# Attention on one core: K and V of a pair of heads loaded in 2 KB rows in one row order, one transfer each

## Chip, cores and metric

The kernel runs on one core of one Trainium2 chip. The metric is device time in microseconds (us) of one launch; the span in the profile is the time from the first to the last instruction of one profiled execution. "PE" is TensorE, "ACT" ScalarE, "DVE" VectorE, "POOL" GpSimd and "SP" SyncE, whose queue issues every transfer here.

## The reference

Softmax attention over 16 x 32 = 512 heads, each with 192 queries and 1024 keys of width 128, in bf16:

```python
B, H, Sq, Sk, D = 16, 32, 192, 1024, 128
def reference(q, k, v):
    scale = q.shape[-1] ** -0.5
    scores = jnp.einsum("bhqd,bhkd->bhqk", q, k) * scale
    p = _softmax(scores, axis=-1)
    return jnp.einsum("bhqk,bhkd->bhqd", p, v)
```

K and V are 134 MB each, Q and the output 25 MB each. Every K and V element is read once.

## The kernel before

The 512 heads go in 256 pairs, p = 0 to 255; x = 0 or 1 is the head within the pair. T = 8 blocks of 128 keys make up a head. All the work of `_attention_kernel` is written out as one instruction stream for each engine, tied together by semaphores; there is no planner.

**Loads (SP, lines 474 to 535).** `load_k(p)` (L479) brings the K of a pair, 512 KB, into one of R = 4 buffers of `kn`, which is 128 partitions x 4 KB. The two heads are read as one run of 128 rows of 4 KB: partition m + 64x would hold 16 consecutive keys of head x. `load_q(p)` (L487) is a transposing transfer of 96 KB into one of 4 buffers of `qt`. `load_v(p)` (L496) brings the V of a pair, also 512 KB, into one of NVS = 10 buffers of `vs`, in two transfers: the first (w = 0) writes partitions 0 to 63, the second (w = 1) partitions 64 to 127. Each moves, for 64 partitions, one 2 KB row from each head (8 consecutive keys); a head's rows go alternately to w = 0 and w = 1. Both add 16 to the same semaphore, so that its reader waits for 32 for each use. `store(g)` (L509) writes the output of four pairs, 384 KB, in rows of 768 bytes.

The order on SP's queue is K, Q of pair n + 4, V of pair n + 8, for every n, and a store after every fourth. K(p) waits until the transposes of pair p - 4 are done, Q(p) until the scores of pair p - 4 are, V(p) until the second product of pair p - 10 is. Before the loop, four K, four Q and all ten V buffers are filled: V(2) to V(9) stand in a row in front of K(4).

**PE (lines 554 to 641).** For every pair PE transposes K in two halves y (`tr`, L569: 16 transposes of 64 columns from `kn` into the single PSUM tile `k_ps`), computes the scores of a head (`qk`, L590: 20 matmuls into `s_ps[x]`) and multiplies by V (`pv`, L608: 48 matmuls for a pair, in two halves of 24). `step(n)` interleaves them in two halves: qk of head 2n, tr(n+1, 1), half of pv(n-2); then qk of head 2n+1, tr(n+2, 0), the other half of pv(n-2). `take(s, c)` (L558) is PE's wait: it waits for the semaphore and counts it down. Only tr with y = 0 takes the semaphore of a K transfer; every tr but the first also takes the one of DVE's copy of the tile before. The steps of the middle run in a hardware loop of four steps.

**The rest.** DVE copies a transposed half from PSUM to `kt` (L656) and normalises the output of a pair (L667, L671). ACT takes the exponential of a head's scores (L707). POOL copies a pair's V from `vs` into `vp` (L549), which has a column of ones behind each block, so that the second product also yields the softmax's sums; it waits for V at L546. In `kt` block 8y + t holds the transposed half y of `kn`: a column of it is a partition of `kn`. In before a column below 64 belongs to head 0 and one from 64 on to head 1, so `qk` picks the head by the columns (64x) and the row group w by the block (8w + t). Since the partition of the scores is the partition that `vs` has for the same key, the key order of K after the transposes has to be the key order of V.

Of the kernel before, what the change touches and what calls it, by code (L numbers as in the profile page):

```python
# [392 lines left out]
                    exp_first(u)  # L393


RS_LO = 2.0 ** -40
RS_HI = 2.0 ** 20
U32 = mybir.dt.uint32
PE_LOOP = 4
HINT = False  # L400


def _attention_kernel(nc, q, k, v, out, NVS=10):
# [5 lines left out]
    T = SK // 128  # L409
    scale = float(D) ** -0.5  # L410
    R = PE_LOOP
# [7 lines left out]
    kf = k.rearrange("b h s d -> (b h) s d")  # L419
    vf = v.rearrange("b h s d -> (b h) s d")  # L420
    of = out.rearrange("b h s d -> (b h) s d")

    with ExitStack() as outer:
        redo = outer.enter_context(nc.sbuf_tensor("redo", [1, 1], mybir.dt.int32))

        def sem(name):
            return outer.enter_context(nc.semaphore(name))
# [4 lines left out]
        s_v = [sem("f_v%d" % i) for i in range(NVS)]  # L432
# [13 lines left out]
        with ExitStack() as es:  # L446
            def sb(name, shape, dt):
                return es.enter_context(nc.sbuf_tensor(name, shape, dt))
# [5 lines left out]
            kn = sb("f_kn", [128, R, 2 * T * D], BF16)  # L454

            kt = sb("f_kt", [128, R, 2 * T, 128], BF16)
            qt = sb("f_qt", [128, R, 3, 128], BF16)

            vs = sb("f_vs", [128, NVS, 2, T * D], BF16)
# [14 lines left out]
            @block.sync  # L474
            def _(e):
                def load_k(p):
                    if p >= R:
                        e.wait_ge(s_tr, 2 * (p - R) + 2)
                    e.dma_start(  # L479
                        kn[:, p % R, :],  # L480
                        kf[2 * p:2 * p + 2].rearrange("x (m s) d -> (x m) (s d)", s=2 * T),
                    ).then_inc(s_kn[p % R], 16)

                def load_q(p):
                    if p >= R:
                        e.wait_ge(s_qk, 2 * (p - R) + 2)
                    e.dma_start_transpose(  # L487
                        qt[:, p % R, :, :],
                        qf[2 * p:2 * p + 2].rearrange("g (p j) d -> (g p) (j d)", j=3),
                    ).then_inc(s_q[p % R], 16)  # L490

                def load_v(p):
                    if p >= NVS:
                        e.wait_ge(s_pv, p - NVS + 1)
                    for w in range(2):
                        e.dma_start(  # L496
                            vs[64 * w: 64 * w + 64, p % NVS, :, :],
                            vf[2 * p:2 * p + 2].rearrange("x (m w t) d -> w m x (t d)", w=2, t=T)[w],
                        ).then_inc(s_v[p % NVS], 16)

                def store(g):
                    so = g % NSO
                    h0 = 2 * GP * g
                    last = GP * (g + 1) == NPR
                    if last:
                        e.wait_ge(s_fin, 1)
                    else:
                        e.wait_ge(s_rc, GP * (g + 1) + 1)
                    e.dma_start(  # L509
                        of[h0:h0 + 2 * GP].rearrange("(a x) (p j) d -> (x p) a (j d)", x=2, j=3),  # L510
                        ob[:, so, :, :],
                    ).then_inc(s_st[so], 16)

                load_k(0)
                load_q(0)
                load_k(1)
                load_q(1)
                load_v(0)
                for p in range(2, R):
                    load_k(p)  # L520
                    load_q(p)
                    load_v(p - 1)
                for p in range(R - 1, min(NVS, NPR)):
                    load_v(p)
                for n in range(NPR + 2):
                    if n + R < NPR:
                        load_k(n + R)
                        load_q(n + R)
                    if n >= 2 and n - 2 + NVS < NPR:
                        load_v(n - 2 + NVS)  # L530
                    if n >= 3 and (n - 2) % GP == 0:
                        store((n - 2) // GP - 1)
                store(NPR // GP - 1)
                for so in range(min(NSO, NPR // GP)):
                    e.wait_ge(s_st[so], 16 * len(range(so, NPR // GP, NSO)))

            @block.gpsimd
            def _(gp):
                gp.memset(ones[:], 1.0).then_inc(s_set, 1)  # L539
                gp.wait_ge(s_set, 1)  # L540
                gp.affine_select(  # L541
                    ident[:], ones[:], [[1, 128]], ALU.is_equal, 0.0, base=0, channel_multiplier=-1
                ).then_inc(s_set, 1)
                gp.memset(vp[:, :, :, D:VB], 1.0).then_inc(s_set, 1)  # L544
                for p in range(NPR):
                    gp.wait_ge(s_v[p % NVS], 32 * (p // NVS + 1))  # L546
                    if p >= R:
                        gp.wait_ge(s_pv, p - R + 1)
                    gp.tensor_copy(  # L549
                        vp[:, p % R, :, 0:D].bitcast(U32),  # L550
                        vs[:, p % NVS, :, :].rearrange("p x (t d) -> p (x t) d", d=D).bitcast(U32),
                    ).then_inc(s_vp, 1)

            @block.tensor
            def _(pe):

                def take(s, c):
                    pe.wait_ge(s, c).then_inc(s, -c)  # L558
# [15 lines left out]
                def qk(h):  # L574
                    p, x = divmod(h, 2)
                    if x == 0:
                        take(s_q[p % R], 16)
                        if p == NPR - 1:
                            take(s_ev, 1)
                    if h >= 2:  # L580
                        take(s_exp, 1)
                    S = s_ps[x]
                    ins = None
                    for t in range(T):
                        cut = {2: (0, 2, 3), 5: (0, 1, 3)}.get(t, (0, 3))
                        for j0, j1 in zip(cut[:-1], cut[1:]):
                            mv = qt[:, p % R, j0:j1, 64 * x: 64 * x + 64]
                            c0 = t * SQ + j0 * 64
                            for w in range(2):
                                ins = pe.matmul(  # L590
                                    S[64 * w: 64 * w + 64, c0: c0 + (j1 - j0) * 64],
                                    kt[:, p % R, 8 * w + t, 64 * x: 64 * x + 64], mv,
                                    start=True, stop=True, tile_position=(0, 64 * w))
                    ins.then_inc(s_qk, 1)

# [21 lines left out]
                def step(n):  # L617
                    for x in range(2):
                        if n < NPR:
                            qk(2 * n + x)  # L620
                        if n + 1 + x < NPR:
                            tr(n + 1 + x, 1 - x)
                        if n >= 2:
                            pv(n - 2, 12 * x, 12 * x + 12)
# [7 lines left out]
                loops = (NPR - 5) // R  # L632
                with nc.Fori(0, loops, engines=[mybir.EngineType.PE], hint_back_edge=HINT,
                             head_slot={mybir.EngineType.PE: 0}):
# [9 lines left out]
            def _(dve):  # L644
                cnt = [0]

                def done(ins):
                    ins.then_inc(s_dv, 1)
                    cnt[0] += 1
                    dve.wait_ge(s_dv, cnt[0])  # L650
# [27 lines left out]
                def check(lo, hi, i):  # L678
                    done(dve.tensor_scalar(chk[:, lo:hi], rinv[:, lo:hi], 1.0 / RS_HI, 1.0 / RS_LO, ALU.max, ALU.min))  # L679
                    done(dve.tensor_tensor(chk[:, lo:hi], chk[:, lo:hi], rinv[:, lo:hi], ALU.not_equal))  # L680
                    done(dve.tensor_reduce(bad[:, i: i + 1], chk[:, lo:hi], mybir.AxisListType.X, ALU.max))  # L681
# [66 lines left out]
```

## Time and profile before

| | us |
|---|---|
| median of three runs | 1199.38 |
| lowest, highest | 1196.12, 1203.05 |
| profiled execution, whole | 1199.44 |
| its span | 1197.7 |
| PE busy in the span | 995.0 |
| ACT, DVE, POOL busy | 744.1, 546.4, 268.1 |

The busy times are sums over the span. A wait shows as idle time ahead of an instruction, with what ended it; `PEq L558` means that the wait of PE's own queue at line 558 (`take`) ended last. A "window" is a stretch of the span, in us from its start; for each the trace gives the busy time of the engines (with the number of instructions), PE's granted clock as a fraction of full speed, the mean busy share of the 16 DMA engines (overlapping packets count twice, so that it can go over 1) and the GB/s that they moved.

### The profile page before, as it was taken

How to read it: one execution, taken by the hardware profiler on the slowest of the kernel's cores; microseconds unless marked ns; L12 is line 12 of the kernel's file. 1: busy time of each engine (PE TensorE's matmuls, PEld its weight loads, DVE VectorE, ACT ScalarE, POOL GpSimd, SP SyncE). 2: the span in 40 equal slices, each digit the busy share in tenths (PEclk: the TensorE clock that was granted, in tenths of full speed). 3: DMA queues.
4: the chain of work that ended last, by engine and by line, in shares of the span. 5: the costliest groups of instructions: out<-in, count | busy, mean ns of one | idle time of the engine just before them, and what ended most of it. 6: DMA issues, size and time to landing. Idle time of an engine off the chain costs nothing. (4 is left out here: it accounts for less than half of the span.)

```text
span 1197.7 us, 67883 instructions
## 1 busy us (share of the span) xinstructions
PE 995.0 (83%) x30722; PEld 947.9 (79%) x30722; DVE 546.4 (46%) x1031; ACT 744.1 (62%) x513; POOL 268.1 (22%) x263
## 2 busy tenths in 40 slices
PE   4598888888888888888888888888888888888885
PEld 3598888887888887887887887787887887878885
DVE  1254444444444444444444444444444444444443
ACT  3276666666666666666666665666666666666663
POOL 1122222222222222222222222222222222222220
PEclk9799999999999999999999999999999999999999
DMA  9999999999999999999999999999999999999991
GB/s 211 230 257 264 284 264 279 277 273 277 282 278 268 277 271 279 275 278 272 280 278 274 277 279 266 281 279 267 285 277 269 284 272 274 275 271 277 274 294 40
DMA packets 250932, 319.39 MB, mean 267 GB/s; under 512 B 119808, under 2 KB 152576, under 8 KB 250880
## 3 DMA queue, kind: packets, MB, share of 16 engines
q1 hardware_dynamic: 250880, 318.85, 104.6%
q8 instruction: 13, 0.21, 0.1%
q14 instruction: 39, 0.32, 0.1%
HBM read 268.44 MB, written 25.17 MB: 245 GB/s over the span
## 5 line engine op out<-in xcount | busy, mean ns | idle before, releaser
L707 ACT ACTIVATE f_pt<-f_s 128x1536 bf16<-128x1536 f32 x512 | 742.8, 1451 | 439.2 <-PE f_s L590 439.2
L656 DVE COPY f_kt<-f_k 128x1024 bf16<-128x1024 bf16 x512 | 354.2, 692 | 623.6 <-PE f_k L569 623.5
L569 PE MATMUL f_k<-f_ident,f_kn 128*64 128x128 bf16 x8192 | 331.2, 221 | 186.2 <-PEq L558 186.0
L549 POOL COPY f_vp<-f_vs 128x1024 uint32<-128x1024 uint32 x256 | 267.2, 1044 | 908.9 <-PE f_o L608 890.3
L608 PE MATMUL f_o<-f_vp,f_pt 128*64 128x129 bf16 x12288 | 459.3, 221 | 2.2 <-PEq L558 2.2
L569 PEld LDWEIGHTS f_k<-f_ident,f_kn 128*64 128x64 bf16 x8192 | 276.1, 110 | 232.1 <-issue 232.0
L590 PE MATMUL f_s<-f_qt,f_kt 128*64 128x192 bf16 (+2 forms) x10240 | 444.4, 231 | 5.2 <-issue 5.2
L608 PEld LDWEIGHTS f_o<-f_vp,f_pt 128*64 128x64 bf16 x12288 | 395.8, 110 | 2.7 <-issue 2.7
L590 PEld LDWEIGHTS f_s<-f_qt,f_kt 128*64 128x64 bf16 x10240 | 360.4, 111 | 5.7 <-issue 5.7
L671 DVE TENSOR_TENSOR f_ob<-f_o,f_rinv 128x384 bf16<-128x384 f32 x256 | 142.7, 557 | 8.9
L667 DVE RECIPROCAL f_rinv<-f_o 128x3 f32<-128x3 f32 x256 | 46.3, 181 | 11.0 <-PE f_o L608 8.5
L707 ACT ACT_TABLE_LOAD x1 | 1.3, 1283 | 0.8 <-PEq L733 0.8
L640 PE MATMUL f_o<-f_bad,f_ones 128*1 128x1 bf16 x1 | 0.2, 164 | 1.4 <-DVEq L696 1.4
L640 PEld LDWEIGHTS f_o<-f_bad,f_ones 128*1 128x1 bf16 x1 | 0.1, 79 | 1.6 <-DVEq L696 1.6
L680 DVE TENSOR_TENSOR f_chk<-f_chk,f_rinv 128x750 f32<-128x750 f32 (+1 forms) x2 | 1.1, 558 | 0.1
L681 DVE TENSOR_REDUCE f_bad<-f_chk 128x1 bf16<-128x750 f32 (+1 forms) x2 | 1.1, 555 | 0.1
L679 DVE TENSOR_SCALAR f_chk<-f_rinv 128x750 f32<-128x750 f32 (+1 forms) x2 | 1.0, 509 | 0.0
L541 POOL TENSOR_SCALAR_AFFINE_SELECT f_ident<-f_ones 128x128 bf16<-128x128 bf16 x1 | 0.3, 294 | 0.1
L698 DVE CAST redo<-f_o 1x1 int32<-1x1 f32 x1 | 0.1, 146 | 0.3 <-PE f_o L641 0.3
L539 POOL MEMSET f_ones<- 128x128 bf16 x1 | 0.2, 205 | 0.3 <-POOLq L733 0.3
L544 POOL MEMSET f_vp<- 128x128 bf16 x1 | 0.2, 213 | 0.0
L733 POOL MEMSET const-float32-0.0<- 128x1 f32 x1 | 0.1, 99 | 0.3 <-issue 0.3
(5 smaller groups left out, 0.5 us busy)
## 6 DMA issues: line engine op xcount, KB each, us to landing
f_kn<-in_k_dram SPq DMA_DIRECT2D x256, 512.0 KB, 9.9
f_vs<-in_v_dram SPq DMA_DIRECT2D x512, 256.0 KB, 9.2
out_dram<-f_ob SPq DMA_DIRECT2D x64, 384.0 KB, 9.5
f_qt<-in_q_dram SPq DMA_TRANSPOSE x256, 9.9
```

The costliest lines, as they stand in the source:

```text
L549: gp.tensor_copy(vp[:, p % R, :, 0:D].bitcast(U32), vs[:, p % NVS, :, :].rearrange("p x (t d) -> p (x t) d", d=D).bitcast(U32),).then_inc( ...
L569: ins = pe.transpose(k_ps[64 * z: 64 * z + 64, t * 128: t * 128 + 128], kn[:, p % R, c0: c0 + 64], ident[:], tile_position=(0, 64 * z))
L590: ins = pe.matmul(S[64 * w: 64 * w + 64, c0: c0 + (j1 - j0) * 64], kt[:, p % R, 8 * w + t, 64 * x: 64 * x + 64], mv, start=True, stop=True ...
L608: ins = pe.matmul(o_ps[64 * x: 64 * x + 64, j * 129: j * 129 + 129], pt[:, (2 * p + x) % NP, t * SQ + j * 64: t * SQ + j * 64 + 64], vp[:, ...
L640: pe.matmul(o_ps[0:1, 0:1], ones[:, 0:1], bad[:, 0:1], start=True, stop=False)
L656: dve.tensor_copy(kt[:, p % R, 8 * y: 8 * y + 8, :], k_ps[:].rearrange("d (t c) -> d t c", c=128),).then_inc(s_ev, 1)
L667: dve.reciprocal(ri, O[:, :, 128]).then_inc(s_rc, 1)
L671: dve.tensor_tensor(ob[:, so, a, :].rearrange("p (j d) -> p j d", j=3), O[:, :, 0:128], ri.unsqueeze(2).to_broadcast([128, 3, D]), ALU.mul ...
L679: done(dve.tensor_scalar(chk[:, lo:hi], rinv[:, lo:hi], 1.0 / RS_HI, 1.0 / RS_LO, ALU.max, ALU.min))
L680: done(dve.tensor_tensor(chk[:, lo:hi], chk[:, lo:hi], rinv[:, lo:hi], ALU.not_equal))
L681: done(dve.tensor_reduce(bad[:, i: i + 1], chk[:, lo:hi], mybir.AxisListType.X, ALU.max))
L707: act.activation(pt[:, h % NP, :], s_ps[h % 2][:], ACT_FN.Exp, scale=scale).then_inc(s_exp, 1)
```

## The change

K is read so that partition m gets one 2 KB row (8 consecutive keys) of each of the two heads: 256 rows of 2 KB instead of 128 of 4 KB, still one transfer over 128 partitions. V is read in the same row order, with one transfer over 128 partitions instead of two over 64 each; its rows stay 2 KB. POOL waits for 16 per use instead of 32. In `kt` the half y is now head y, so `qk` picks the head by the block (8x + t) and the row group by the columns (64w). `HINT` moves to another line with the same value.

```diff
                     e.dma_start(
-                        kn[:, p % R, :],
-                        kf[2 * p:2 * p + 2].rearrange("x (m s) d -> (x m) (s d)", s=2 * T),
+                        kn[:, p % R, :].rearrange("m (x c) -> m x c", x=2),
+                        kf[2 * p:2 * p + 2].rearrange("x (m t) d -> m x (t d)", t=T),
                     ).then_inc(s_kn[p % R], 16)
...
-                    for w in range(2):
-                        e.dma_start(
-                            vs[64 * w: 64 * w + 64, p % NVS, :, :],
-                            vf[2 * p:2 * p + 2].rearrange("x (m w t) d -> w m x (t d)", w=2, t=T)[w],
-                        ).then_inc(s_v[p % NVS], 16)
+                    e.dma_start(
+                        vs[:, p % NVS, :, :],
+                        vf[2 * p:2 * p + 2].rearrange("x (m t) d -> m x (t d)", t=T),
+                    ).then_inc(s_v[p % NVS], 16)
...
-                    gp.wait_ge(s_v[p % NVS], 32 * (p // NVS + 1))
+                    gp.wait_ge(s_v[p % NVS], 16 * (p // NVS + 1))
...
-                                    kt[:, p % R, 8 * w + t, 64 * x: 64 * x + 64], mv,
+                                    kt[:, p % R, 8 * x + t, 64 * w: 64 * w + 64], mv,
```

## Rows read from the trace of the kernel before

**Rows 1.** Page parts 1 and 3: engines' busy time, the packets, the DMA queue.
```profile
PE 995.0 (83%) x30722; PEld 947.9 (79%) x30722; DVE 546.4 (46%) x1031; ACT 744.1 (62%) x513; POOL 268.1 (22%) x263
DMA packets 250932, 319.39 MB, mean 267 GB/s; under 512 B 119808, under 2 KB 152576, under 8 KB 250880
q1 hardware_dynamic: 250880, 318.85, 104.6%
```
**Rows 2.** PE's waits from 100 to 1100 us: us in total, times, longest us.
```profile
PE f_k L569 <- PEq L558: 144.3, 219, 2.0
```
**Rows 3.** DMA issues by line from 100 to 1100 us: count, KB each, median us to landing.
```profile
f_kn<-in_k_dram SPq DMA_DIRECT2D x221, 512.0 KB, 9.9
```
**Rows 4.** Timeline of PE, 598 to 618 us: start, us, instructions [idle before, releaser].
```profile
600.09 0.86 PE L590 MATMUL f_s<-f_qt,f_kt 128*64 128x192 bf16 x20
601.36 0.64 PE L569 MATMUL f_k<-f_ident,f_kn 128*64 128x128 bf16 x16 [0.41 <-PEq L558]
602.54 0.86 PE L590 MATMUL f_s<-f_qt,f_kt 128*64 128x192 bf16 x20
...
604.36 0.86 PE L590 MATMUL f_s<-f_qt,f_kt 128*64 128x192 bf16 x20
```
**Rows 5.** Timeline of PE, 38 to 88 us.
```profile
40.38 1.06 PE L569 MATMUL f_k<-f_ident,f_kn 128*64 128x128 bf16 x16 [17.64 <-PEq L558]
...
42.51 1.52 PE L590 MATMUL f_s<-f_qt,f_kt 128*64 128x192 bf16 x20
...
52.86 0.64 PE L590 MATMUL f_s<-f_qt,f_kt 128*64 128x64 bf16 x13 [1.38 <-issue]
...
59.49 0.52 PE L590 MATMUL f_s<-f_qt,f_kt 128*64 128x192 bf16 x9 [2.63 <-issue]
...
62.85 0.86 PE L590 MATMUL f_s<-f_qt,f_kt 128*64 128x192 bf16 x20
...
83.02 0.86 PE L590 MATMUL f_s<-f_qt,f_kt 128*64 128x192 bf16 x20
```
**Rows 6.** Timeline, 1174 to 1200 us: the last scores.
```profile
1181.80 0.86 PE L590 MATMUL f_s<-f_qt,f_kt 128*64 128x192 bf16 x20
```
**Rows 7.** Timeline of SP, 0 to 110 us.
```profile
10.98 11.27 SPq L496 DMA_DIRECT2D f_vs<-in_v_dram  x16
22.30 0.59 SPq L479 DMA_DIRECT2D f_kn<-in_k_dram  x1
```
**Rows 8.** Windows: us, busy of five engines, PE's clock, DMA share, GB/s; startup.
```profile
20.00:24.00 4.00, 2.75 (x69) 2.53 (x63) 0.69 (x1) 2.67 (x2) 1.84 (x2) 0.84 1.07 213
...
28.00:32.00 4.00, 0.00 (x0) 0.00 (x0) 0.00 (x0) 0.00 (x0) 0.00 (x0) 0.51 1.09 217
32.00:36.00 4.00, 0.00 (x0) 0.00 (x0) 0.00 (x0) 0.00 (x0) 0.00 (x0) 0.50 1.07 214
```
**Rows 9.** Windows of 0.5 us in the steady part, same columns.
```profile
608.00:608.50 0.50, 0.50 (x24) 0.50 (x21) 0.46 (x1) 0.50 (x1) 0.06 (x1) 1.00 0.99 393
...
609.50:610.00 0.50, 0.29 (x11) 0.32 (x13) 0.00 (x0) 0.50 (x1) 0.00 (x0) 1.00 1.08 209
610.00:610.50 0.50, 0.50 (x25) 0.50 (x21) 0.11 (x1) 0.50 (x1) 0.00 (x0) 1.00 1.11 209
...
612.00:612.50 0.50, 0.50 (x24) 0.50 (x20) 0.29 (x1) 0.50 (x1) 0.23 (x1) 1.00 1.09 370
612.50:613.00 0.50, 0.50 (x24) 0.50 (x20) 0.40 (x1) 0.50 (x1) 0.00 (x0) 1.00 1.18 449
613.00:613.50 0.50, 0.50 (x18) 0.35 (x13) 0.00 (x0) 0.21 (x1) 0.00 (x0) 1.00 1.11 459
```
**Rows 10.** Timeline, 600 to 610 us, and the page's DMA issues: the store.
```profile
604.04 0.60 SPq L509 DMA_DIRECT2D out_dram<-f_ob  x1
...
out_dram<-f_ob SPq DMA_DIRECT2D x64, 384.0 KB, 9.5
```
**Rows 11.** SP's issues by line: duration ns min/median/max, first and last start.
```profile
L479 SPq DMA_DIRECT2D f_kn<-in_k_dram x256: 327/596/1222, 0.8 to 1164.0; - x128
L496 SPq DMA_DIRECT2D f_vs<-in_v_dram x512: 596/622/2048, 4.5 to 1150.8; - x171
L509 SPq DMA_DIRECT2D out_dram<-f_ob x64: 395/595/1092, 64.4 to 1189.3; - x64
L487 SPq DMA_TRANSPOSE f_qt<-in_q_dram x256: 1184/1221/5485, 1.3 to 1165.9; - x128
```
**Rows 12.** Landing of K, us min/median/max, in the view of its line.
```profile
DMA to landing us min/median/max: 3.7/9.9/17.8
```

More of the change, by code (lines that the diff above doesn't have):

```diff
@@ L393, in _ @@
                     exp_first(u)
+HINT = False
 RS_LO = 2.0 ** -40
@@ L399 @@
 PE_LOOP = 4
-HINT = False
 def _attention_kernel(nc, q, k, v, out, NVS=10):
```

## The prediction
> **What bounds the kernel now.** The first view is the page's busy time and its DMA rows: PE is busy 995.0 of 1197.7 us, while the DMA queue's packets fill 104.6% of the 16 engines' time [rows 1]. So PE has some 200 us of gaps and the transfers have none. The second view is PE's waits in the steady part: there is one kind only, 219 waits of the transposes of K at L569 for PE's queue at L558, 144.3 us as the profile counts them [rows 2]. Their places are in the timeline: the first transpose after the scores of a pair's second head waits, which is tr(n+2, 0), the one that takes a K transfer; the other half step runs through [rows 4]. The third view gives the pace: 221 K transfers are issued in 1000 us, so a pair takes 1000/221 = 4.52 us now [rows 3].
>
> What would PE do without these waits? There is a stretch early on, after the queue has caught up, where it waits for nothing: from 62.85 to 83.02 us there are 11 half steps, (83.02 - 62.85)/11 = 1.834 us for one and **3.67 us for a pair** [rows 5]. In the steady part the half step without a wait takes 604.36 - 602.54 = 1.82 us and the one with a wait 602.54 - 600.09 = 2.45 us [rows 4], so the free stretch is the same work at the same clock. Nothing else is near 3.67: ACT has 744.1/256 = 2.9 us of work per pair, DVE 2.1, POOL 1.0 [rows 1]. So the kernel is bound by its transfers, 4.52 us a pair, and PE stands 0.85 us behind.
>
> Where do the 4.52 us go? At the start eight V loads, V(2) to V(9), stand in a row, 16 transfers that SP issues from 10.98 us on, and K(4) is issued behind them at 22.30 us [rows 7]. While nothing but V moves, the rate is 213 to 217 GB/s with the DMA engines' share at 1.07 to 1.09 [rows 8]: the engines are full and yet slow. In the steady part the rate goes up and down in each pair: 209 GB/s in the low phase, 393 to 459 in the high one [rows 9]. The low phase is V's, by its rate; the high phase is K with Q behind it. So a V load takes 524,288 B / 214 GB/s = **2.45 us** and a K load of the same bytes 524,288/393 = **1.33 us**. That leaves 4.52 - 2.45 - 1.33 = **0.74 us** for Q (96 KB), a quarter of a store (96 KB) and the seams.
>
> **Why V is slow** decides everything. V differs from K in two ways: its rows are 2 KB instead of 4 KB, and one transfer writes 64 partitions instead of 128. The change takes the second away and gives K the first. A third kind of transfer separates the two: the store moves rows of 768 bytes, 152,576 - 119,808 = 32,768 packets [rows 1], over all 128 partitions. One is issued at 604.04 us and lands, at the median, 9.5 us later, at about 613.5 [rows 10]; between the low phase and K's, the window at 612.0 us runs at 370 GB/s [rows 9], which I read as its second part. Rows shorter than V's then reach 370 GB/s when 128 partitions take part. So I put V's slowness down to the 64 partitions. The Trainium skill agrees with that part: "SBUF — State Buffer", section "Door 1: The DMA port swizzle", says that partitions 0 to 63 reach only 8 of the 16 ports to this memory, and measures 196 GB/s against 328 GB/s with all 128 at 1 MiB; the trace has 214 and 393 GB/s for V and K, so the trace agrees that half the partitions cost about half the rate, and its upper rate is higher.
>
> **The change part by part.**
> V in one transfer over 128 partitions: no row shows 2 KB rows over 128 partitions. Its bounds are K's 1.33 us (128 partitions, longer rows) and today's 2.45 us (same rows, 64 partitions). At the store's 370 GB/s it would be 1.42 us. I take 1.33, since by the argument above the partitions matter and the rows don't. It saves 1.12 us a pair of transfer.
> K in 256 rows of 2 KB: bounds 1.33 us (as today) and 2.45 us (as today's V). No gain beyond 1.33 is allowed for, as its partitions stay. I take 1.33.
> So the transfers of a pair need 1.33 + 1.33 + 0.74 = **3.40 us**, less than PE's 3.67. With 370 GB/s for both it would be 2 x 1.42 + 0.74 = 3.58, still less. PE takes over as the bound, and the saving per pair is 4.52 - 3.67 = 0.85 us, not 1.12.
> SP's issues: one V issue of about 0.62 us goes away. K's keeps its 0.6 us: the store, with 512 rows, is issued in 0.595 us, K with 128 in 0.596 [rows 11], so rows don't lengthen it. SP then needs 0.60 + 1.22 + 0.62 + 0.60/4 = 2.6 us a pair, under 3.67. The waits on SP stay where they are. What is late next could be K, behind V on SP's queue: V(n+8) waits for the second product of pair n - 2, which ends with step n; K(n+5) follows it and is needed in the second half of step n + 3, 2.5 steps or 9.2 us later. K now lands 9.9 us after issue with the queue full and 3.7 us at the least [rows 12]; with a queue that drains faster than it is filled, it has at most V (1.33) and a store (393,216 B at 370 GB/s, 1.1) ahead, so about 6 us. It fits with 3 us to spare, and that cover is gone if the transfers need more than 3.67 us.
> PE: `qk` reads other columns of `kt`, with the same number and shapes of matmuls and the same waits; POOL waits for one transfer instead of two: nothing, up or down.
> Start: ten V loads stand ahead of K(4), each 1.12 us shorter, 11 us at most; PE's wait of 17.64 us that ends at 40.38 us [rows 5] ends some 11 us sooner, with K(4) issued sooner too, as SP issues 8 V transfers instead of 16.
>
> **The sum**, against the profiled execution. From the scores of head 6 at 42.51 us [rows 5] to those of the last head at 1181.80 us [rows 6] there are 505 half steps, 1139.3 us. At 1.834 us they take 926.2 us, and with the two waits inside the scores that no transfer causes (1.38 + 2.63 [rows 5]) 930.2: 209 us less. What lies behind the last scores, 1197.7 - 1181.8 = 15.9 us, stays. 1197.7 - 209 - 11 = 977.7 us of span. The whole execution is 1.7 us longer than its span and lies on the median (1199.44 against 1199.38). That gives 979.4, **980 us**.
>
> **The rivals.**
> The transfers still bound. They do so if 2 KB rows run under 1,048,576 B / (3.67 - 0.74) us = 358 GB/s. For: 393 GB/s is from one clean window, and the store's 370 is near. Against: K's windows go up to 459 [rows 9]. At 330 GB/s a pair takes 2 x 1.59 + 0.74 = 3.92 us, 0.25 more than PE: 980 + 256 x 0.25 = 1044 us. The skill's page above gives 328 GB/s for 128 partitions; by that figure the time, an estimate, would be about this rival's.
> Row length is the cause. Then V's 214 GB/s comes from 2 KB rows; V gains nothing and K falls from 1.33 to 2.45 us. A pair takes 4.52 + 1.12 = 5.64 us and the kernel 1199 + 256 x 1.12 = 1486 us. It ends slower than now as soon as K and V run under 1,048,576/(2.45 + 1.33) = 277 GB/s. For: V has the shorter rows and the lower rate. Against: the store's rows at 370. "Perfetto Trace Analysis" in the Trainium skill, section "DMA Optimizations", speaks for it: going from 2 KB to 4 KB pieces can improve throughput much where a kernel is bound by transfers, and this change goes the other way for K; the store's window disagrees.
> The merge doesn't do what it says: V's rate is set by reading two heads 256 KB apart for one partition. Then V stays at 2.45, and K, which now reads so too, falls likewise: the same 1486 us. If only V stays and K too, it is 1199.
>
> **How the numbers follow.** PE takes over, 965 to 1000 us: 0.72. Transfers still bound, 1000 to 1120: 0.19. No change: 0.03. Slower, about 1486: 0.06. The range 960 to 1055 us holds the first case and the better part of the second. Faster by over 0.5% is 0.91, within 0.5% (about what a measurement can tell from no change here) 0.03, slower 0.06.
>
> **What would show it.** Right: the waits at L569 in the steady part shrink from 144 us to nearly nothing, half steps are 1.82 to 1.85 us throughout, PE is busy over 95% of the span, no window of V shows 210 GB/s any more, the mean rate rises to about 319 MB/980 us = 326 GB/s and the DMA share falls below 1; the long first wait ends near 29 us. Wrong: waits at L569 with high and low phases gone mean the second case; a steady rate near 210 GB/s means the third.

## The result and the profile after

The changed kernel takes **982.62 us** (median; 981.78 to 983.79) against 1199.53 us for the kernel before beside it: a ratio of 0.8192, 95% interval 0.8167 to 0.8218. The forecast was 980 us, with a range of 960 to 1055. The lines of the code lie one lower: L568 is the K transpose (L569 before), L557 the wait `take` (L558), L589 the scores (L590).

The page of the changed kernel, the parts of [rows 1] (busy time of the engines, packets, DMA queue) and the DMA issues (count, KB each, median us to landing):

```profile
PE 948.1 (97%) x30722; PEld 945.6 (96%) x30722; DVE 546.1 (56%) x1031; ACT 743.6 (76%) x513; POOL 267.7 (27%) x263
...
DMA packets 279602, 319.35 MB, mean 325 GB/s; under 512 B 115712, under 2 KB 148480, under 8 KB 279552
q1 hardware_dynamic: 279552, 318.84, 102.5%
...
f_kn<-in_k_dram SPq DMA_DIRECT2D x256, 512.0 KB, 5.9
```

PE is busy 97% of the span instead of 83%. The same bytes move at 325 GB/s instead of 267, and K lands 5.9 us after its issue instead of 9.9.

PE's two largest waits in the whole span of the changed kernel (us in total, times, longest), which answer to [rows 2]:

```profile
PE f_k L568 <- PEq L557: 18.5, 8, 9.6
PE f_s L589 <- issue: 4.2, 1, 4.2
```

Half of the 18.5 us is one wait at the start; from 100 to 900 us the view of PE's waits is empty. The windows of the changed kernel (us, busy of five engines, PE's clock, DMA share, GB/s), two from the start, where V loads stand in a row as in [rows 8], the whole steady part, and then three half microseconds in it as in [rows 9]:

```profile
20.00:24.00 4.00, 0.00 (x0) 0.00 (x0) 0.00 (x0) 1.25 (x1) 0.71 (x1) 0.97 1.06 386
24.00:27.00 3.00, 0.00 (x0) 0.00 (x0) 0.00 (x0) 0.00 (x0) 0.00 (x0) 0.50 1.04 383
...
100.00:850.00 750.00, 750.00 (x24549) 750.00 (x24544) 434.03 (x819) 593.12 (x410) 213.47 (x205) 1.00 1.07 340
...
491.50:492.00 0.50, 0.50 (x22) 0.50 (x18) 0.00 (x0) 0.28 (x1) 0.00 (x0) 1.00 1.36 134
492.00:492.50 0.50, 0.50 (x24) 0.50 (x21) 0.00 (x0) 0.33 (x1) 0.00 (x0) 1.00 0.57 160
...
494.00:494.50 0.50, 0.50 (x25) 0.50 (x21) 0.13 (x2) 0.48 (x1) 0.46 (x1) 1.00 1.01 373
```

The same 750 us of the kernel before:

```profile
100.00:850.00 750.00, 641.62 (x19908) 610.90 (x19903) 352.20 (x664) 481.69 (x333) 173.28 (x166) 1.00 1.08 276
```

Where V had moved at 213 to 217 GB/s, it moves at 383 to 386. In the steady part the long low phase is gone. Around 492 us 365 to 381 GB/s is the usual rate, and what is left are lows of about a microsecond in some of the pairs (134 and 160 GB/s here); from 100 to 850 us one half microsecond in ten is under 240 GB/s. PE is busy in all of the 750 us, at a granted clock of 1.00 (2.4 GHz). The DMA share has hardly moved, 1.07 against 1.08: it says how long packets were under way, not how many bytes they carried.

The timeline of PE in the changed kernel, the places of [rows 5] and [rows 6]:

```profile
29.37 1.07 PE L568 MATMUL f_k<-f_ident,f_kn 128*64 128x128 bf16 x16 [9.60 <-PEq L557]
...
31.50 1.52 PE L589 MATMUL f_s<-f_qt,f_kt 128*64 128x192 bf16 x20
...
48.48 0.85 PE L589 MATMUL f_s<-f_qt,f_kt 128*64 128x192 bf16 x9 [4.24 <-issue]
...
966.15 0.86 PE L589 MATMUL f_s<-f_qt,f_kt 128*64 128x192 bf16 x20
```

The first long wait ends at 29.37 us, 11.0 us sooner than before. From the scores of head 6 to those of the last head the 505 half steps take 966.15 - 31.50 = 934.7 us, 1.851 each; before it was 1139.3.

### The profile page after: what moved, and what is told of

It reads as the page before. It is cut to its first block, busy times and chain, and to the rows that moved or that the text cites. A ratio compares the mean times of both kernels' runs of the same rounds, so it can differ in the third digit from the quotient of the medians.

```text
span 982.0 us, 67627 instructions
## 1 busy us (share of the span) xinstructions
PE 948.1 (97%) x30722; PEld 945.6 (96%) x30722; DVE 546.1 (56%) x1031; ACT 743.6 (76%) x513; POOL 267.7 (27%) x263
## 5 line engine op out<-in xcount | busy, mean ns | idle before, releaser
L589 PE MATMUL f_s<-f_qt,f_kt 128*64 128x192 bf16 (+2 forms) x10240 | 443.5, 231 | 4.2 <-issue 4.2
L589 PEld LDWEIGHTS f_s<-f_qt,f_kt 128*64 128x64 bf16 x10240 | 359.8, 111 | 4.5 <-issue 4.5
L568 PE MATMUL f_k<-f_ident,f_kn 128*64 128x128 bf16 x8192 | 331.3, 220 | 18.5 <-PEq L557 18.5
L568 PEld LDWEIGHTS f_k<-f_ident,f_kn 128*64 128x64 bf16 x8192 | 288.3, 111 | 20.0 <-issue 19.8
L680 DVE TENSOR_REDUCE f_bad<-f_chk 128x1 bf16<-128x750 f32 (+1 forms) x2 | 1.1, 555 | 0.1
L678 DVE TENSOR_SCALAR f_chk<-f_rinv 128x750 f32<-128x750 f32 (+1 forms) x2 | 1.0, 508 | 0.0
```

Of the source, the lines that this page charges most:

```text
L568: ins = pe.transpose(k_ps[64 * z: 64 * z + 64, t * 128: t * 128 + 128], kn[:, p % R, c0: c0 + 64], ident[:], tile_position=(0, 64 * z))
L589: ins = pe.matmul(S[64 * w: 64 * w + 64, c0: c0 + (j1 - j0) * 64], kt[:, p % R, 8 * x + t, 64 * w: 64 * w + 64], mv, start=True, stop=True ...
```

## Experiments

The theory: V was slow because each of its transfers wrote only 64 partitions; over 128 it runs at K's rate, and PE becomes the bound. The rivals: V was slow because of its 2 KB rows or their order, or because there were two transfers; and, for the new bound, that the transfers are still at their limit. Ratios are against the kernel before, run beside each group on the same chip (medians 1199.77, 1200.06 and 1199.84 us).

| kernel | V: partitions, rows | K: partitions, rows | us | ratio, 95% interval |
|---|---|---|---|---|
| before | 64, 2 KB | 128, 4 KB | 1199.5 | 1 |
| changed | 128, 2 KB | 128, 2 KB | 982.6 | 0.8192 (0.8167 to 0.8218) |
| e1 | 64, 2 KB | 128, 2 KB | 1217.7 | 1.0147 (1.0118 to 1.0176) |
| e2 | 128, 2 KB, one head each | 128, 2 KB | 982.5 | 0.8187 (0.8167 to 0.8208) |
| e3 | 128, 2 KB | 128, 4 KB | 983.0 | 0.8201 (0.8173 to 0.823) |
| e4 | 64, 4 KB | 128, 2 KB | 1202.3 | 1.0016 (1.0001 to 1.0031) |
| e9 | 128, 2 KB | 64, 2 KB | 1209.9 | 1.0088 (1.0058 to 1.0118) |

**e1: K's part alone.** V goes back to two transfers over 64 partitions, in the new row order.

```diff
-                    e.dma_start(
-                        vs[:, p % NVS, :, :],
-                        vf[2 * p:2 * p + 2].rearrange("x (m t) d -> m x (t d)", t=T),
-                    ).then_inc(s_v[p % NVS], 16)
+                    for w in range(2):
+                        e.dma_start(
+                            vs[64 * w: 64 * w + 64, p % NVS, :, :],
+                            vf[2 * p:2 * p + 2, 512 * w: 512 * w + 512].rearrange("x (m t) d -> m x (t d)", t=T),
+                        ).then_inc(s_v[p % NVS], 16)
```

> The changed kernel with V again in two transfers over partitions 0 to 63 and 64 to 127, in the new row order and 2 KB rows; K stays changed. So this is K's part of the change alone. If the 64 partitions made V slow, V needs 2.45 us of transfer again and the time goes back to that of the kernel before, 1190 to 1200 us, with windows near 214 GB/s. If V was slow because of its old row order (a step of 4 KB between the rows of a partition's neighbours), V keeps the full rate: 983 us. If 2 KB rows cost K anything over 4 KB ones, the time is above 1200 us: 1486 at the worst.

Measured: 1217.7 us, so nothing of the gain is left, and the row order isn't the cause. The startup shows V's old rate (same columns as above):

```profile
28.00:32.00 4.00, 0.00 (x0) 0.00 (x0) 0.00 (x0) 0.00 (x0) 0.00 (x0) 0.50 1.07 214
```

It is also 1.5% slower than before: the expected 1190 to 1200 us was wrong by 18 us, as in the expectation's last case. K's half-length rows are the likely cause; e6 tries that alone.

**e2: two transfers of 256 KB, each over 128 partitions.**

```diff
+                    for x in range(2):
+                        e.dma_start(
+                            vs[:, p % NVS, x, :],
+                            vf[2 * p + x].rearrange("(m t) d -> m (t d)", t=T),
+                        ).then_inc(s_v[p % NVS], 16)
```

> The changed kernel with V in two transfers of 256 KB each, as before, but each over all 128 partitions: one for each head, one 2 KB row per partition. If the 64 partitions made V slow: 983 us within 0.5%, since SP's second issue of 0.6 us a pair lies beside PE's 3.67 us. If it was the number or the size of the transfers (256 KB instead of 512): back towards 1199 us, at least 1050.

Measured: 982.5 us, the changed kernel's time. Neither the number nor the size of the transfers matters here, nor that one transfer reads two heads; the second issue on SP costs nothing.

**e3: V's part alone.** K's load and the indices of the scores are those of before.

```diff
-                        kn[:, p % R, :].rearrange("m (x c) -> m x c", x=2),
-                        kf[2 * p:2 * p + 2].rearrange("x (m t) d -> m x (t d)", t=T),
+                        kn[:, p % R, :],
+                        kf[2 * p:2 * p + 2].rearrange("x (m s) d -> (x m) (s d)", s=2 * T),
...
-                                    kt[:, p % R, 8 * x + t, 64 * w: 64 * w + 64], mv,
+                                    kt[:, p % R, 8 * w + t, 64 * x: 64 * x + 64], mv,
```

> The changed kernel with K's part undone: K in 128 rows of 4 KB as before and the scores' indices as before; V in one transfer. It is V's part of the change alone. The scores' rows then stand in another key order than V's, so each probability meets another key's value: the same amount of work on other data. If K's rows cost nothing and PE is the bound: 983 us within 0.5%. If K's 2 KB rows hold the changed kernel up: less than 975 us.

Measured: 983.0 us. All of the gain is V's part. K's part has no time of its own in the changed kernel: it is there so that K's keys stand in the order that one V transfer over 128 partitions gives.

**e4: 64 partitions with 4 KB rows.**

```diff
+                    for x in range(2):
+                        e.dma_start(
+                            vs[64 * x: 64 * x + 64, p % NVS, :, :].rearrange("m a c -> m (a c)"),
+                            vf[2 * p + x].rearrange("(m s) d -> m (s d)", s=2 * T),
+                        ).then_inc(s_v[p % NVS], 16)
```

> The changed kernel with V in two transfers over 64 partitions each, now in 4 KB rows: partitions 0 to 63 take head 0, 64 to 127 head 1. The keys in vs then stand in another order and the heads are mixed, so the second product works on other data. It is the fourth corner of partitions (64, 128) against rows (2 KB, 4 KB). If the 64 partitions made V slow: 1190 to 1205 us, as with 2 KB rows. If the row length did: V at K's 1.33 us, 983 us.

Measured: 1202.3 us. K's row length doesn't bring V K's rate, as the startup shows too, with 222 GB/s:

```profile
28.00:32.00 4.00, 0.00 (x0) 0.00 (x0) 0.00 (x0) 0.00 (x0) 0.00 (x0) 0.50 1.05 222
```

Against e1 the longer rows give 15 us, a fifteenth of what the partitions give (1217.7 - 982.6 = 235).

**e9: the same on K.** K in two transfers over 64 partitions each (`kn[64 * w: 64 * w + 64, ...]`, keys 512w to 512w + 511 of both heads), V in one; `take` waits for 32.

> The changed kernel with K, not V, in two transfers over partitions 0 to 63 and 64 to 127, 2 KB rows, the same row order; V stays in one. If 64 partitions slow any load, K now takes what V took before and the time is that of e1_v_two_halves, 1205 to 1225 us. If the slowness belongs to V's buffers or its reader on POOL, K's split costs nothing: 983 us.

Measured: 1209.9 us. Splitting K by partitions takes the whole gain away again, although V is now whole: the slowness goes with the partitions, not with V, its buffers or POOL. PE again waits at the K transposes (100 to 850 us: total, times, longest):

```profile
PE f_k L569 <- PEq L558: 116.0, 164, 1.8
```

**e5, e6, e7: what the transfers need when PE isn't in the way.** In the changed kernel PE hides what the transfers need. Here PE computes only 2 of the 8 key blocks of the second product, and every transfer stays.

```diff
-                order = [(j, t) for j in range(3) for t in range(T)]
+                TP = 2
+                order = [(j, t) for j in range(3) for t in range(TP)]
...
-                                start=t == 0, stop=t == T - 1, skip_group_check=True,
+                                start=t == 0, stop=t == TP - 1, skip_group_check=True,
...
-                            pv(n - 2, 12 * x, 12 * x + 12)
+                            pv(n - 2, 3 * x, 3 * x + 3)
```

e5 is this edit in the changed kernel:

> The changed kernel with 6 of the 8 key blocks of the second product left out on PE (12 matmuls a pair instead of 48); all transfers stay. PE then needs about 2.6 us a pair and ACT 2.9, so the transfers are to be the bound and their own pace shows. By the prediction's 3.40 us a pair the time is 983 - 252 x 0.27 = 915 us, 900 to 930. If the transfers are at their limit already in the changed kernel (its DMA share is still 1.067): no change, 975 to 983 us. If they are much faster than 3.40 us, ACT binds at about 3.0 us a pair: 815 us.

e6 has e3's edit as well:

> As e5_lite_after (6 of 8 key blocks of the second product left out), with K back in 128 rows of 4 KB, so that the row length is tried where the transfers bind and nothing hides it. If 2 KB rows over 128 partitions cost nothing: the same as e5_lite_after within 1%. If each row has a price: faster than e5_lite_after, by 10% of K's 1.33 us a pair (34 us) or more.

e7 is the edit in the kernel before:

> The kernel before with 6 of the 8 key blocks of the second product left out on PE. If the kernel before is bound by its transfers alone, PE's work is worth nothing there: 1190 to 1200 us. If PE and the transfers hold each other up, so that the 4.52 us a pair are in part PE's: faster by up to 256 x 1 us, 940 to 1150 us.

Measured: e5 929.3 us (0.7747, 0.7732 to 0.7763), e6 915.4 us (0.7627, 0.7613 to 0.7641), e7 1192.5 us (0.9934, 0.9915 to 0.9954). The K issues from 100 to 850 us (count, KB, us to landing) give the pace; e5 first, then e6:

```profile
f_kn<-in_k_dram SPq DMA_DIRECT2D x216, 512.0 KB, 7.8
```
```profile
f_kn<-in_k_dram SPq DMA_DIRECT2D x220, 512.0 KB, 7.9
```

e5's pair takes 750/216 = 3.47 us, and PE waits for K again (66 times from 100 to 850 us, 66.4 us in all); 3.40 was the estimate. So the transfers of the changed kernel have about 3.67 - 3.47 = 0.20 us a pair to spare. e6 is faster than e5 by 13.9 us, 13.9/256 = 0.054 us a pair: that is the price of K's shorter rows, 4% of its 1.33 us, far from the 34 us of the second case and yet, at 1.5%, outside the first. In e7 PE has three quarters of the second product less to do and the kernel gains 7 us of 1200: before, PE's work was all but free.

**e10: what Q costs.** e5 with Q brought by a plain transfer of the same bytes.

```diff
-                    e.dma_start_transpose(
-                        qt[:, p % R, :, :],
+                    e.dma_start(
+                        qt[:, p % R, :, :].rearrange("m j d -> m (j d)"),
```

> As e5_lite_after (6 of 8 key blocks of the second product left out), with Q brought by a plain transfer of the same 96 KB in rows of 768 bytes instead of a transposing one, so that the scores are of other data. It asks what the 0.74 us of the sum are that are neither K nor V. If Q costs its bytes alone (0.25 us at 393 GB/s): the same as e5_lite_after, 925 to 932 us. If the transposing transfer holds the queue up (the rate drops to under 100 GB/s right behind Q's packets): less, down to 815 us, where ACT binds.

Measured: 875.5 us (0.73, 0.7274 to 0.7325), 53.9 us less than e5 (53.6 by the ratios, as the two ran on different chips), 0.21 us a pair. The steady part (same columns as the windows above) runs at 380 GB/s, against 359 in e5, here second:

```profile
100.00:850.00 750.00, 694.28 (x19268) 611.07 (x19262) 465.45 (x919) 648.33 (x459) 239.33 (x229) 1.00 1.05 380
```
```profile
100.00:850.00 750.00, 668.71 (x18161) 575.45 (x18160) 438.82 (x865) 617.66 (x434) 226.27 (x217) 1.00 1.08 359
```

So 0.21 of the 0.74 us that was neither K nor V is the way Q is brought. The lows go with it: a half microsecond of e5 falls to 12 GB/s (509.0 to 509.5 us), while e10 has none below 308 from 490 to 498 us. How the transposing transfer holds the queue up isn't shown.

**e8: another order at the start.** The changed kernel, with V(3) to V(9) behind the loop's K and Q instead of in front of K(4).

```diff
-                for p in range(R - 1, min(NVS, NPR)):
-                    load_v(p)
+                nv = R - 1
...
-                    if n >= 2 and n - 2 + NVS < NPR:
-                        load_v(n - 2 + NVS)
+                    for _ in range(2 - n % 2):
+                        if nv < NPR and nv <= n - 2 + NVS:
+                            load_v(nv)
+                            nv += 1
```

> The changed kernel with another order of the first V loads: V(3) to V(9) no longer stand in front of K(4) but follow the K and Q of the loop, two and one in turn, until V is 8 pairs ahead again. The wait of 9.6 us before the fifth K and most of PE's slow clock behind it should go. Expected 972 us (970 to 976), against 983. If the startup is paid back by waits for K or V later, as the transfers have little room (107% share): no change, 980 to 985 us.

Measured: 980.8 us (0.8172, 0.8161 to 0.8184); the interval overlaps the changed kernel's, so no gain is shown. The expectation of 972 us was wrong. Its timeline at the start (the second line is head 14, which starts at 53.05 us in the changed kernel):

```profile
25.77 1.49 PE L590 MATMUL f_s<-f_qt,f_kt 128*64 128x192 bf16 x20 [4.28 <-PEq L558]
...
49.64 0.86 PE L590 MATMUL f_s<-f_qt,f_kt 128*64 128x192 bf16 x20
```

The wait of 9.6 us for K(4) is gone, but head 6, the first of PE's hardware loop, now waits 4.28 us. Its Q isn't what it waits for: that transfer was issued at 8.04 us and landed 7.6 us later; and ACT was done with head 4, whose tile the scores go into, at 19.04 us. By the profile PE's own queue ended the wait, at the entry of the loop. That the wait for K had hidden this is a reading, and what holds the queue there isn't shown. Head 6 starts 5.7 us sooner, head 14 only 3.4, and the span ends 1.7 us sooner.

## Why the prediction was right, point by point

**What bounds.** Right. The kernel before was bound by its transfers: e7 takes most of the second product off PE and gains 0.6%. The changed one is bound by PE: no wait in 800 us, 205 pairs in 750 us = 3.66 us for each, where 3.67 was read from a free stretch of 20 us in the trace of before.

**Why V was slow.** Right, and now shown by three runs. With 64 partitions a load is slow with 2 KB and 4 KB rows, in either row order and for K as well as V (e1, e4, e9); with 128 it is fast whether the bytes come in one transfer or two (e2). The closest pair is e1 and e2: both bring V in two transfers of 256 KB, 128 rows of 2 KB each, and only the partitions differ, 1217.7 us against 982.5. The prediction had argued from a store, which carries bytes the other way; e2 and e3 show it for loads. That 64 partitions reach half of the ports into the memory is the Trainium skill's account ("SBUF — State Buffer", "Door 1: The DMA port swizzle"); no run here looks at ports. A rule of the Trainium skill in "DMA: Bandwidth & Descriptors", "Rules for kernel authors", that two transfers to disjoint partition halves serialize and one over 128 partitions should be used, agrees: 982.6 us against 1217.7 (e1).

**The terms.** V's 1.33 us held: 524,288 B at the 386 GB/s of the startup window is 1.36. K's price of nothing for its halved rows was too low: e6 shows 0.054 us a pair, 14 us of transfers, and e1's 18 us above before point the same way (V's row order changed there too). The forecast stood because the transfers' 0.20 us of room covers it. The 3.40 us of transfers were 3.47; with K's rows still 4 KB a pair takes 750/220 = 3.41 (e6), so the wrong size was K's term. The rule of the Trainium skill in "Perfetto Trace Analysis", "DMA Optimizations", that spoke against the change has this much in it here: going from 4 KB to 2 KB costs 4% of a K load over 128 partitions.

**The cover.** K's landing time was forecast at about 6 us with 9.2 allowed; it is 5.9. SP's issues were costless, as two V issues cost nothing either (e2).

**The sum.** 505 half steps were put at 930.2 us and took 934.7; the start was put at 11 us and gave 11.0; the tail was left at 15.9 and is 982.0 - 966.15 = 15.9. The sum left out the slow clock after the first wait: the granted clock is 0.50 (1.2 GHz) from 30 to 34 us, and the first half step behind the wait takes 3.0 us in place of 1.83 (the next scores start at 34.52 us). One further wait, of 1.9 us, comes at 956.11 us, and it isn't for K's transfer but for DVE: three instructions that test the range of the softmax's reciprocals (L678 to L680) occupy DVE from 952.44 to 955.24 us, its copy of the K tile follows, and PE's next transposes need that copy done. The kernel before has the same three, with a wait of only 0.52 us behind them; the sum had no term for this. The rest, 1.4 us, lies for the most part around the wait of 4.24 us inside the scores, which was put at 4.0 in two parts; there too the granted clock is 0.50, from 49 to 51 us.

**What was forecast to be seen and wasn't.** The DMA share was to fall below 1 and is 1.07. With transfers needing 3.47 of 3.67 us it was wrong to expect more than a twentieth; overlapping packets count twice, so it can't tell a full queue from a nearly full one. GB/s (276 to 340) and the landing time (9.9 to 5.9 us) can.

**The rivals.** Transfers still binding, put at 0.19, was the near one: 3.47 us is 5% below PE's pace. The slower rival, row length, was wrong in kind: rows cost 4%, where it needed 84% on K's load.

## What to carry to other kernels

When a transfer is slow at a full DMA share, look first at how many partitions one transfer writes and only then at its row length: here 64 instead of 128 partitions cost 45% of the rate and half the row length, over 128, 4%. A layout that makes rows shorter may well pay if it brings all 128 partitions into each transfer, and reordering another operand to match cost no time here: on PE nothing but indices changed, and the transfers had room for the shorter rows (e3). Before counting such a saving whole, read the next bound from a stretch of the old trace where the first one happens to be absent: 20 us of it gave the new time within 0.3%.

## What the runs showed of the hardware that was not expected

- Halving a load's rows from 4 KB to 2 KB over 128 partitions costs 0.054 us of some 1.33 (e5 against e6), where nothing was expected.
- A transposing transfer of 96 KB costs 0.21 us more than a plain one of the same bytes where transfers bind (e5 against e10), and with plain transfers alone the mixed stream keeps 380 GB/s over 750 us.
- K split by partitions (e9, 1209.9 us) seems a little cheaper than V split (e1, 1217.7 us). The intervals of the two ratios meet at 1.0118, so the difference is barely clear of noise, and why it is there is open.
